# Padding 192-byte rows to a 256-byte pitch in SBUF, in a fused linear-attention and MLP kernel

## The chip, the cores and the metric

One core of one Trainium2 chip. The metric is the device time of one execution in microseconds (us), compared by the median and, where kernels were timed in rounds on the same chip, by ratio. The span in a profile is a little shorter than the device time (198.7 against 200.5 us).

## The reference, cut to what matters

```python
# r, k, v, w: (4, 8, 768, 48) float32; u: (8, 48); x @ w_in: 384 -> 2048; @ w_out: 2048 -> 384
for t in range(S):
    cur = einsum('bhd,bhe->bhde', u[None] * kt, vt)
    y[:, :, t] = einsum('bhd,bhde->bhe', rt, state + cur)
    state = wt[:, :, :, None] * state + einsum('bhd,bhe->bhde', kt, vt)
x = y.transpose(0, 2, 1, 3).reshape(B * S, H * D)
h = maximum(x @ w_in, 0); out = (s * h * h + b) @ w_out
```

The attention is computed in 24 chunks of 128 tokens (4 batches, 6 chunks each). For a chunk, each of w, r, k and v is 128 tokens by 8 heads by 48 floats. In HBM the 48 floats (192 bytes) of a token and head are contiguous, so a load is 1024 rows of 192 B.

## The kernel before

A load writes token t to partition t, the eight heads one after another:

```python
if which == 0:
    c["w"] = ain.tile([128, H, D], FP32, name="wt", tag="wt")          # 8 buffers each
elif which == 1:
    c["rk"] = ain.tile([128, 2, H, D], FP32, name="rkt", tag="rkt")
elif which == 3:
    c["v"] = ain.tile([128, H, D], FP32, name="vt", tag="vt")
...
nc.sync.dma_start(out=dst, in_=src[bb, :, t0 : t0 + L, :].transpose([1, 0, 2]))
```

The readers of these buffers are `ln` (ScalarE, w), `rkp` (GpSimd, r times k), `mult` (VectorE, r and k times the decays), and `yd` and the cast of v (GpSimd). All operations go into a plan, which simulates the engines and ring sizes and puts the instructions in order; attention of later chunks is interleaved with the MLP of earlier ones:

```python
pl = Plan(dict(w=8, rk=8, v=8, lw=NLW, prd=NPR, E=2, RK=RKB, ...))
...
add(("load", n, x), "SP", 0.6, load, (n, x), [], take, 10.0 * n + x, dma=1.03)
```

So a ring size in this dictionary changes the order on every engine. The eight pieces of the MLP weights are loaded after chunk 3, and from chunk 16 on two transposes of each chunk go through the DMA queue too (`RK<-prd` and `xT<-x_sb`), behind the loads.

The softmax here doesn't subtract the row's maximum and nothing guards it: scores larger than these inputs give would overflow.

## Time and profile before

| | before |
|---|---|
| device time, median (range of the first 3 runs) | 200.46 us (198.93 to 201.3) |
| span of the profiled run | 198.7 us |
| PE busy, share of the span | 94% |
| packets of 192 B | 98,304, median 15 ns, 95% under 32 ns |
| w load, issue to landing, median | 4.5 us |

The page divides the span into busy time of each engine (PE is TensorE's matmuls, PEld its weight loads, DVE VectorE, ACT ScalarE, POOL GpSimd). In a row of the windows view, "40.00 (x494)" is 40.00 us busy with 494 instructions in that stretch. A timeline row gives start, duration, engine, line, operation and tiles, then in brackets the idle time ahead of it and what ended that. The figures on packets come from the trace's record of every DMA packet (start, duration, size).

### The profile page before, as it was taken

What the parts mean: (1) busy time and instruction counts of PE and PEld (TensorE: products, weight loads), DVE (VectorE), ACT (ScalarE), POOL (GpSimd) and SP (SyncE); (2) the same over time, 40 slices, a digit from 0 to 9 for tenths busy, and PEclk for the clock granted to TensorE, in tenths of its full rate; (3) what the DMA queues carried; (4) which work ended last, traced back from release to release, by engine and by line L of the source; (5) the groups of instructions that cost most, each with busy time, mean ns of one, the idle gap of its engine ahead of it and who ended that gap; (6) DMA issues with size and microseconds to landing.
All of it is one profiled execution on the core that took longest, in us unless ns stands there. A gap on an engine that the chain in (4) does not pass through costs nothing.

```text
span 198.7 us, 4921 instructions
## 1 busy us (share of the span) xinstructions
PE 187.0 (94%) x1928; PEld 138.9 (70%) x1928; DVE 133.1 (67%) x212; ACT 133.2 (67%) x240; POOL 114.4 (58%) x144
## 2 busy tenths in 40 slices
PE   6997888979999999999999999999999999999992
PEld 4766567745668777777776786776687778777651
DVE  6476838836977978869787686799787692222221
ACT  3446487745658999999996997690069868768000
POOL 3787932029998899959987788959981000000000
PEclk9999999999999999999999999999999999999999
DMA  6999999979999999999999899999433931111122
GB/s 125 200 175 179 299 394 371 278 145 200 188 156 197 160 195 173 200 234 195 220 169 194 186 202 190 210 236 173 128 82 75 122 98 27 43 40 40 43 79 79
DMA packets 119239, 33.29 MB, mean 168 GB/s; under 512 B 112432, under 2 KB 117680, under 8 KB 119216
## 3 DMA queue, kind: packets, MB, share of 16 engines
q1 hardware_dynamic: 119216, 32.98, 83.0%
q8 instruction: 15, 0.25, 0.6%
q14 instruction: 8, 0.07, 0.1%
HBM read 25.36 MB, written 4.72 MB: 151 GB/s over the span
## 4 chain that ended last, share of the span: by engine, by line
PE 66%; DMA 14%; SPq 11%; ACT 3%; POOL 2%; issue 2%; DVE 1%; POOLq 0%
PE o_ps L584 26%; PE h_ps L546 23%; SPq L225 9%; DMA wi_st<-in_moe_w_in_dram 5%; DMA wt<-in_w_dram 5%; DMA rkt<-in_k_dram 4%; PE mt_ps L382 3%; PE o_psh L584 3%; PE trps L340 2%; PE y_ps L419 2%; PE y_ps L410 2%; PE cums L281 1%; PE cums L284 1%; PE d_ps L435 1%; ACT rh L559 1%
## 5 line engine op out<-in xcount | busy, mean ns | idle before, releaser
L546 PE MATMUL h_ps<-xT,w_in 128*128 128x256 bf16 x576 | 73.9, 273 | 2.0 <-ACT w_in L634 1.4
L559 ACT ACTIVATE rh<-h_ps 128x512 bf16<-128x512 f32 x96 | 56.2, 598 | 23.2 <-PE h_ps L546 21.8
L584 PE MATMUL o_ps<-w_out,gT 128*128 128x384 bf16 x352 | 66.3, 326 | 0.0
L546 PEld LDWEIGHTS <-w_in 128*128 128x128 bf16 x576 | 53.7, 98 | 12.5 <-issue 1.8
L584 PEld LDWEIGHTS <-gT 128*128 128x128 bf16 x384 | 35.8, 98 | 19.2
L571 DVE TENSOR_TENSOR gT<-rh 128x512 bf16<-128x512 bf16 x56 | 29.4, 537 | 14.5 <-ACT rh L559 14.4
L237 POOL TENSOR_TENSOR rkp<-rkt 128x384 f32<-128x384 f32 x24 | 25.1, 1047 | 17.2 <-DMA rkt<-in_k_dram 17.1
L394 DVE TENSOR_TENSOR mt_sb<-mt_ps,tri_strict 128x1024 bf16<-128x1024 f32 x24 | 29.2, 1216 | 1.3 <-PE mt_ps L382 1.3
L268 POOL TENSOR_TENSOR yd<-vt,cd 128x384 bf16<-128x384 f32 x24 | 25.2, 1048 | 4.8 <-DVE cd L262 4.6
L313 DVE TENSOR_TENSOR prd<-rkt,E 128x768 bf16<-128x768 f32 x24 | 24.1, 1004 | 5.6 <-ACT E L303 4.1
L569 ACT ACTIVATE gT<-rh 128x512 bf16<-128x512 bf16 x40 | 25.2, 630 | 1.3
L248 POOL TENSOR_TENSOR rku<-rkp,u_bc 128x384 f32<-128x384 f32 x24 | 24.6, 1025 | 0.4
L303 ACT ACTIVATE E<-cums 128x768 bf16<-128x768 f32 x24 | 19.4, 806 | 7.5 <-PE cums L289 7.4
L594 DVE SCALAR_TENSOR_TENSOR o_sb<-o_ps,s_bc,bconst 128x384 f32<-128x384 f32 x22 | 13.5, 615 | 14.8 <-PE o_ps L584 13.4
L486 POOL TENSOR_TENSOR st<-stmp,l 128x384 bf16<-128x384 bf16 x16 | 18.6, 1164 | 8.3 <-DVE stmp L477 7.9
L355 ACT COPY RK<-trps 128x1024 bf16<-128x1024 bf16 x16 | 16.1, 1008 | 5.5 <-PE trps L340 5.5
L449 DVE TENSOR_TENSOR x_sb<-y_ps,yd 128x384 bf16<-128x384 f32 x24 | 13.3, 552 | 6.7 <-PE y_ps L419 5.2
L262 DVE TENSOR_REDUCE cd<-rku 128x8 f32<-128x384 f32 x24 | 13.0, 542 | 6.8 <-POOL rku L248 6.8
L232 ACT ACTIVATE logw<-wt 128x384 bf16<-128x384 f32 x24 | 12.4, 523 | 7.0 <-DMA wt<-in_w_dram 6.8
L816 PE MATMUL warm_ps<-warm_sb 128*128 128x256 bf16 x104 | 15.1, 294 | 1.1 <-DVE warm_sb L795 1.1
L636 POOL CAST vb<-vt 128x384 bf16<-128x384 f32 x24 | 13.4, 558 | 0.0
L816 PEld LDWEIGHTS <-warm_sb 128*128 128x128 bf16 x104 | 10.2, 105 | 2.7 <-DVE warm_sb L795 1.1
(52 smaller groups left out, 168.5 us busy)
## 6 DMA issues: line engine op xcount, KB each, us to landing
wt<-in_w_dram SPq DMA_DIRECT2D x24, 192.0 KB, 4.5
rkt<-in_r_dram SPq DMA_DIRECT2D x24, 192.0 KB, 4.4
rkt<-in_k_dram SPq DMA_DIRECT2D x24, 192.0 KB, 4.6
vt<-in_v_dram SPq DMA_DIRECT2D x24, 192.0 KB, 4.4
out_dram<-o_sb SPq DMA_DIRECT2D x24, 192.0 KB, 2.2
wi_st<-in_moe_w_in_dram SPq DMA_DIRECT2D x4, 768.0 KB, 8.3
wo_st<-in_moe_w_out_dram SPq DMA_DIRECT2D x4, 768.0 KB, 7.6
u_bc<-in_u_dram SPq DMA_DIRECT2D x1, 192.0 KB, 4.3
```

The lines of the kernel that those rows point to most:

```text
L237: nc.gpsimd.tensor_tensor(out=rkp, in0=c["rk"][:, 0].rearrange("t h d -> t (h d)"), in1=c["rk"][:, 1].rearrange("t h d -> t (h d)"), op=AL ...
L248: nc.gpsimd.tensor_tensor(out=rku.rearrange("t h d -> t (h d)"), in0=c["rkp"], in1=u_bc, op=ALU.mult)
L268: nc.gpsimd.tensor_tensor(out=yd, in0=c["v"], in1=c["cd"].unsqueeze(2).to_broadcast([128, H, D]), op=ALU.mult,)
L303: nc.scalar.activation(out=E, in_=ps[:, :, 0:HD], func=AF.Exp)
L313: nc.vector.tensor_tensor(out=prd[:, :, :, 0:D].rearrange("t x h d -> t (x h) d"), in0=c["rk"].rearrange("t x h d -> t (x h) d"), in1=c["E ...
L394: nc.vector.tensor_tensor(out=m.rearrange("s g p t -> s (g p) t"), in0=c["mt_ps"].rearrange("s g p t -> s (g p) t"), in1=tri_strict.unsque ...
L546: nc.tensor.matmul(ps[:, f, :], lhsT=w_in_sb[ft // FPP][:, kt, (ft % FPP) * 128 : (ft % FPP + 1) * 128], rhs=xT[T][:, kt, :], start=(f == ...
L559: nc.scalar.activation(out=rh, in_=hs[T, i], func=AF.Relu)
L569: nc.scalar.activation(out=g, in_=rh, func=AF.Square)
L571: nc.vector.tensor_tensor(out=g, in0=rh, in1=rh, op=ALU.mult)
L584: nc.tensor.matmul(ps, lhsT=gT[T][:, ft, tt * 128 : (tt + 1) * 128], rhs=w_out_sb[ft // FPP][:, ft % FPP, :], start=(ft == 0), stop=(ft == ...
L816: nc.tensor.matmul(warm_ps, lhsT=warm_sb[:, 0:128], rhs=warm_sb, start=True, stop=True)
```

## The change

The intent: rows padded to 256 B in SBUF, so that each 192-byte descriptor lands aligned. As the padded buffers are larger, w gets 5 of them and v gets 7, and the plan is told so.

```diff
-            c["w"] = ain.tile([128, H, D], FP32, name="wt", tag="wt")
+            c["w"] = ain.tile([128, H, 64], FP32, name="wt", tag="wt", bufs=5)[:, :, 0:D]
-            c["rk"] = ain.tile([128, 2, H, D], FP32, name="rkt", tag="rkt")
+            c["rk"] = ain.tile([128, 2, H, 64], FP32, name="rkt", tag="rkt")[:, :, :, 0:D]
-            c["v"] = ain.tile([128, H, D], FP32, name="vt", tag="vt")
+            c["v"] = ain.tile([128, H, 64], FP32, name="vt", tag="vt", bufs=7)[:, :, 0:D]
... (pool1 and pool1b: the same products, written with h and d apart)
-        dict(w=8, rk=8, v=8, lw=NLW, ...
+        dict(w=5, rk=8, v=7, lw=NLW, ...
```

More of the change, by code (lines that the diff above doesn't have):

```diff
@@ L235, in pool1 @@
         c = cb[n]
-        rkp = work.tile([128, HD], FP32, name="rkp", tag="rkp", bufs=2)
+        rkp = work.tile([128, H, D], FP32, name="rkp", tag="rkp", bufs=2)
         nc.gpsimd.tensor_tensor(
             out=rkp,
-            in0=c["rk"][:, 0].rearrange("t h d -> t (h d)"),
-            in1=c["rk"][:, 1].rearrange("t h d -> t (h d)"),
+            in0=c["rk"][:, 0],
+            in1=c["rk"][:, 1],
             op=ALU.mult,
@@ L248, in pool1b @@
         nc.gpsimd.tensor_tensor(
-            out=rku.rearrange("t h d -> t (h d)"), in0=c["rkp"], in1=u_bc, op=ALU.mult
+            out=rku.rearrange("t h d -> t (h d)"),
+            in0=c["rkp"].rearrange("t h d -> t (h d)"),
+            in1=u_bc,
+            op=ALU.mult
         )
@@ L623 @@
     pl = Plan(
-        dict(w=8, rk=8, v=8, lw=NLW, prd=NPR, E=2, RK=RKB, M=3, vb=6, yd=6, x=XSB,
+        dict(w=5, rk=8, v=7, lw=NLW, prd=NPR, E=2, RK=RKB, M=3, vb=6, yd=6, x=XSB,
              cd=4, rkp=2, rku=2, l2=5, A=1, B=2, h=2, o=2, gT=3, xT=XTB, rh=4,
```

## The prediction

0 us for packets, 0 for engine reads, 0 for rings and 0.4 for the order make 200.46 into 200.9, said as 200.8. The "it" of the two checks is the idea that rows off a 256 B boundary cost more. A line through the medians of 65 ns at 1536 B and 84 at 2048 B gives about 15 ns at 192 B (an estimate: 65 less 1344/512 of 19), which is the median measured, so I held that there was nothing left to save. The "floor" of 15 ns is that median (72% of the packets took 13 to 16 ns), and the 0 to +20 ns for an engine's read was a guess.

> **What bounds the kernel now.** I read the windows view first, which gives the busy time of each engine by stretch (its order in a row: PE, PEld, DVE, ACT, POOL, then clock, DMA share, GB/s).
>
> ```profile
> 0.00:20.00 20.00, 17.01 (x178) 12.49 (x179) 12.28 (x24) 9.03 (x15) 13.17 (x24) 1.00 0.97 170
> 20.00:50.00 30.00, 25.90 (x246) 18.66 (x244) 19.42 (x34) 19.69 (x33) 14.22 (x16) 1.00 1.00 281
> 50.00:90.00 40.00, 40.00 (x494) 30.67 (x489) 33.12 (x50) 34.67 (x67) 34.96 (x44) 1.00 1.13 187
> 90.00:110.00 20.00, 19.03 (x221) 14.73 (x219) 16.39 (x26) 17.64 (x36) 17.73 (x22) 1.00 1.15 198
> 110.00:140.00 30.00, 30.00 (x321) 22.33 (x319) 24.09 (x37) 21.47 (x42) 25.33 (x30) 1.00 1.07 196
> 140.00:190.00 50.00, 50.00 (x458) 37.16 (x457) 26.01 (x44) 30.76 (x51) 8.95 (x12) 1.00 0.31 70
> ```
>
> From 50 to 190 us PE idles for 1.0 us (the second row from 90). The DMA engines are full too until 140. Since a busy PE is not a PE at its peak, I checked in the timeline of PE that its groups stand end to start:
>
> ```profile
> 81.33 0.82 PE L546 MATMUL h_ps<-xT,w_in 128*128 128x256 bf16 x6
> 81.99 0.81 PE L584 MATMUL o_ps<-w_out,gT 128*128 128x384 bf16 x4
> 82.73 0.40 PE L382 MATMUL mt_ps<-RK 48*128 48x128 bf16 x8
> 83.06 0.82 PE L584 MATMUL o_ps<-w_out,gT 128*128 128x384 bf16 x4
> 83.72 0.61 PE L340 MATMUL trps<-identity,prd 128*128 128x128 bf16 x8
> ```
>
> Starts are 0.66 us apart after six h_ps (0.109 us a matmul) and four o_ps (0.163 us). With such spacings for every kind, the matmuls in program order after 49.73 us (the mt_ps of chunk 4) sum to about 142.6 us; they end at 195.1, 145.4 us later. So some 3 us of that stretch are stalls. The span of 198.7 us is then: **49.7** us until PE is saturated, **145.4** of nearly solid PE, **3.6** for the last eviction and store. The loads can matter in two ways: through the first term, and by falling behind in the second.
>
> How far ahead they are, from the timelines of the DMA queue and of ScalarE:
>
> ```profile
> 45.32 0.73 SPq L225 DMA_DIRECT2D wt<-in_w_dram  x1
> 49.58 0.52 ACT L232 ACTIVATE logw<-wt 128x384 bf16<-128x384 f32 x1 [0.69 <-DMA wt<-in_w_dram]
> ...
> 103.47 0.94 SPq L225 DMA_DIRECT2D wt<-in_w_dram  x1
> 108.05 0.52 ACT L232 ACTIVATE logw<-wt 128x384 bf16<-128x384 f32 x1 [1.69 <-DMA wt<-in_w_dram]
> ```
>
> For chunk 6, w is issued at 45.3 and read at 49.6, as soon as it lands; for chunk 19 it is 103.5 and 108.1, again with a wait. In between the lead is 4 to 10 us, of which 4.5 are the landing. So loads are **just in time** all the way: they cost PE nothing now, faster ones would give it nothing after 50 us, but clearly slower ones would pass through to it.
>
> [...] Two checks before believing that it binds here:
>
> First, the packet records of the trace. Of 98,304 packets of 192 B, the median took 15 ns, and 72% took 13 to 16 ns. Other median lengths are 18 ns at 256 B, 65 at 1536 B and 84 at 2048 B. [...] The slow 28% (18 to 36 ns) are not particular rows either: several loads that ran with little else in flight have under 2% of them, others 70%, and both kinds follow each other at about 1.0 us a load. I read these as two loads sharing an engine.
>
> Second, the addresses in the built programs. Before, every w, r, k and v buffer begins 224 B past a 256 B boundary, so rows stand 224, 160, 96 and 32 B past one, and three of four cross a boundary. After, the pitch is 256 B but the buffers still begin 224 B past a boundary: **every** row spans 224 to 416 and crosses. The stated intent is not what the program does. [...] The source rows in HBM are as before.
>
> [...] rkp reads flat rows and yd an 8x48 pattern with a broadcast, for the same time.
>
> ```profile
> L237 POOL TENSOR_TENSOR rkp<-rkt 128x384 f32<-128x384 f32 x24 | 25.1, 1047 | 17.2 <-DMA rkt<-in_k_dram 17.1
> L268 POOL TENSOR_TENSOR yd<-vt,cd 128x384 bf16<-128x384 f32 x24 | 25.2, 1048 | 4.8 <-DVE cd L262 4.6
> L636 POOL CAST vb<-vt 128x384 bf16<-128x384 f32 x24 | 13.4, 558 | 0.0
> ```
>
> **The change part by part.**
>
> - *Packets.* Same number, size and source. My estimate of the saving per packet is 0 ns, so loads stay at 64 packets per engine of about 16 ns, 1.03 us. Start: 16 loads before the weights, unchanged, 0 us. Even if every packet took 15 ns (0.96 us a load), 16 loads would give 1.1 us and the first loads after the weights 0.5.
> - *Engine reads.* ln 24 x 523 ns, mult 24 x 1004, rkp 24 x 1047, yd 24 x 1048 and the cast of v 24 x 558 now read at a 256 B pitch. ln and mult already write 64-element rows. I put each at 0 to +20 ns: 24 x 3 x 20 ns is at most 1.4 us on GpSimd, which idles over 3 us in every ten. On the path: 0.
> - *Rings.* w goes from 8 buffers to 5 and v from 8 to 7, which can hold a load back. As loads run at most two or three chunks ahead, the reader that frees the fifth w buffer back is long done: the smallest margin in the trace before is 13 us (w of chunk 14, issued at 80.2 or 15 at 85.4, against the ln of chunks 9 and 10, done at 66.7 and 71.9). For v, seven back, it is 9.4 us (chunk 23: issued at 126.7, chunk 16's yd done at 117.3). No new wait: 0.
> - *Order.* The kernel plans its own order from those rings, so the order changes although the diff does not show it. Comparing the built programs: all engines are the same up to about the load of chunk 12 (some 75 us into the span); after that three stores move ahead of loads and PE interleaves attention and MLP otherwise. PE has the same matmuls. The stores that move up wait for o_sb evictions that ended by 68.5 us in the trace before, so the queue should not block on them. In the tail, the first h_ps of token pair 10 stands about 4.7 us of PE work after the y_ps that it depends on (5.0 before), and that way goes through an addition (0.55), and a DMA transpose (2.3 us to landing). It fits, barely. I allow -1 to +2.5 us, centre +0.4.
>
> Sum: 0 + 0 + 0 + 0.4, so 200.46 becomes 200.9; I say **200.8 us**.
>
> **The rivals.** (1) *Aligned writes were the cost.* Then some of the DMA-full stretch shortens: speaking for it, the DMA share over 1.0 from 50 to 140 and the slow 28%. Against: 15 ns is already the floor, the rows do not become aligned, and PE is solid from 50 us on, so only the start could gain: 1 to 2 us, 199. (2) *The crossing costs on the write side*, now in all rows. [...] Against: the median does not spread over four values[...]. (3) *The new order stalls PE.* The order before was tuned with its rings; a worse fit around the two DMA transposes of the tail, or ScalarE as the bound (34.67 of 40 us from 50 to 90), would make 202 to 204. (4) *The new order is luckier*: at most the 3 us of stalls that are left, 198.
>
> **Range and chances.** Repeated runs of the kernel before spread from 198.93 to 201.3. Adding the order's -1 to +2.5 and some weight for rival 2 gives **197.8 to 204.2**. Faster by over 2% needs 4 us, more than PE's stalls hold unless the start shrinks as well: **0.04**. Slower by over 2% needs rival 2 or a bad case of rival 3: **0.11**. Within 2%: **0.85**.
>
> **What would show it.** Right: 192 B packets still with a median of 15 ns, loads landing in about 4.5 us, weights' first matmul near 25.7 us, PE busy over 138 of 140 us from 50 to 190, GpSimd's means within 20 ns of 1047, 1048 and 558. Rival 1: packets under 15 ns and the chunk 4 cums before 43 us. Rival 2: packets of 17 ns or more, cums of chunk 4 past 46 us, more wait of ScalarE's ln on wt. Rival 3: the start alike and holes in PE after 75 us, with another engine or the transposes as their releaser. A result above 204 or below 197.8 makes me wrong, most likely in the packet term.

## The result, and the profile after

The changed kernel took **213.07 us** (211.91 to 213.5, 4 runs) beside 200.03 us for the kernel before (4 runs): ratio **1.064**, 95% interval 1.056 to 1.072. Ratios here are the mean time of one kernel's fast runs over that of the other's from the same rounds, so not quite the ratio of the medians quoted. The result is correct. The forecast was 200.8 us, with 204.2 as the upper end: clearly wrong.

The windows view of the changed kernel, same stretches and columns as in the prediction:

```profile
0.00:20.00 20.00, 17.88 (x158) 12.83 (x158) 11.50 (x23) 7.57 (x13) 13.11 (x24) 1.00 1.10 154
20.00:50.00 30.00, 24.53 (x244) 18.11 (x244) 18.47 (x33) 19.79 (x33) 12.14 (x15) 1.00 1.01 278
50.00:90.00 40.00, 38.68 (x461) 28.87 (x459) 32.60 (x47) 31.76 (x59) 34.89 (x42) 1.00 1.10 175
90.00:110.00 20.00, 17.76 (x187) 13.85 (x184) 12.32 (x18) 16.60 (x33) 12.03 (x17) 0.91 1.24 177
110.00:140.00 30.00, 28.35 (x305) 20.95 (x302) 23.03 (x37) 24.36 (x47) 27.58 (x34) 1.00 1.15 180
140.00:190.00 50.00, 47.83 (x470) 36.00 (x471) 31.32 (x48) 28.75 (x48) 15.06 (x17) 0.97 0.44 95
```

PE now idles for 7.4 us between 50 and 190 us (1.32 + 2.24 + 1.65 + 2.17), where it idled for 1.0. The DMA engines are about as full as before (shares of 1.10, 1.24 and 1.15 from 50 to 140 us, 1.13, 1.15 and 1.07 before) but move less in the stretches of loads: 175 against 187 GB/s from 50 to 90, 177 against 198, 180 against 196. And the granted clock of PE, 1.00 throughout before, falls to 0.91 and 0.97 in two rows.

The loads themselves, from the DMA queue's timeline of the changed kernel:

```profile
51.78 1.14 SPq L225 DMA_DIRECT2D wt<-in_w_dram  x1
52.97 1.09 SPq L225 DMA_DIRECT2D rkt<-in_r_dram  x1
...
91.30 1.76 SPq L611 DMA_DIRECT2D out_dram<-o_sb  x1
93.16 0.39 SPq L225 DMA_DIRECT2D wt<-in_w_dram  x1
```

In the steady stretch an issue now follows the last after about 1.17 us (it was about 1.03, as at 62.43, 63.53, 64.52 and 65.53 us before): the issues go at about the rate at which such loads drain (1.15 us a load in e1_micro below). From chunk 5 to chunk 23, the w loads were issued 4.64 us apart on average before and 5.04 us after. The last line is the w load of chunk 15, which stands behind a store; e2_align0 below, which has the same order, issues it at 83.47 us, 9.7 us earlier, while its PE is only 4.8 us ahead just before this place.

PE and ScalarE of the changed kernel, at that same w load:

```profile
93.60 1.47 PE L549 MATMUL h_ps<-xT,w_in 128*128 128x256 bf16 x12
...
97.00 0.52 ACT L232 ACTIVATE logw<-wt 128x384 bf16<-128x384 f32 x1 [1.88 <-DMA wt<-in_w_dram]
98.06 2.31 PE L549 MATMUL h_ps<-xT,w_in 128*128 128x256 bf16 x12 [2.14 <-ACT rh L562]
```

`ln` waits 1.88 us for w; the relu behind it on the same engine starts only after it, at 97.43, though the h_ps before it were done at 95.1; and the matmuls that need the relu's buffer wait 2.14 us. The late load reaches PE through an operation that has nothing to do with it. Those twelve h_ps then take 2.31 us, where the twelve at 93.60 took 1.47. In a windows view by 1 us the granted clock is 0.76 from 98 to 99, 0.50 from 99 to 101, 0.53 from 101 to 102, and 1.00 on either side. Half the clock for 3.4 us costs about 1.7 us (an estimate: half of 3.4, the sum of those shortfalls over 0.5).

Over the whole span ScalarE idled for w for 6.8 us before and 13.2 us after (the last number of a row of the lines view, first the kernel before, then the changed one):

```profile
L232 ACT ACTIVATE logw<-wt 128x384 bf16<-128x384 f32 x24 | 12.4, 523 | 7.0 <-DMA wt<-in_w_dram 6.8
L232 ACT ACTIVATE logw<-wt 128x384 bf16<-128x384 f32 x24 | 12.4, 522 | 13.2 <-DMA wt<-in_w_dram 13.2
```

Finally the medians of the DMA issues (out and in, number, KB, us from issue to landing), first before, then after; all four loads land half a microsecond or more later:

```profile
wt<-in_w_dram SPq DMA_DIRECT2D x24, 192.0 KB, 4.5
rkt<-in_r_dram SPq DMA_DIRECT2D x24, 192.0 KB, 4.4
rkt<-in_k_dram SPq DMA_DIRECT2D x24, 192.0 KB, 4.6
vt<-in_v_dram SPq DMA_DIRECT2D x24, 192.0 KB, 4.4
```

```profile
wt<-in_w_dram SPq DMA_DIRECT2D x24, 192.0 KB, 5.0
rkt<-in_r_dram SPq DMA_DIRECT2D x24, 192.0 KB, 5.2
rkt<-in_k_dram SPq DMA_DIRECT2D x24, 192.0 KB, 5.2
vt<-in_v_dram SPq DMA_DIRECT2D x24, 192.0 KB, 5.0
```

Yet the median packet of 192 B still took 15 ns. What grew is the tail: packets over 16 ns went from 28 to 39%, and the mean from 18.2 to 20.6 ns.

### The profile page after: what moved, and what is told of

The parts are those of the page before. It is cut to its first block, busy times and chain, and to the rows that moved or that the text cites. A ratio compares the mean times of both kernels' runs of the same rounds, so it can differ in the third digit from the quotient of the medians.

```text
span 211.2 us, 4914 instructions
## 1 busy us (share of the span) xinstructions
PE 192.6 (91%) x1928; PEld 141.9 (67%) x1928; DVE 134.2 (64%) x212; ACT 134.3 (64%) x240; POOL 114.8 (54%) x144
## 4 chain that ended last, share of the span: by engine, by line
PE 47%; SPq 20%; DMA 19%; ACT 8%; issue 3%; POOL 1%; DVE 0%
PE o_ps L587 20%; PE h_ps L549 18%; SPq L225 18%; DMA wt<-in_w_dram 9%; DMA wi_st<-in_moe_w_in_dram 5%; DMA RK<-prd 4%; ACT rh L562 4%; PE o_psh L587 2%; PE mt_ps L385 2%; ACT RK L358 2%; PE y_ps L422 1%; SPq L520 1%; PE y_ps L413 1%; PE trps L343 1%; ACT gT L572 1%
## 5 line engine op out<-in xcount | busy, mean ns | idle before, releaser
L587 PE MATMUL o_ps<-w_out,gT 128*128 128x384 bf16 x352 | 68.1, 331 | 0.0
L549 PEld LDWEIGHTS <-w_in 128*128 128x128 bf16 x576 | 55.1, 99 | 16.4 <-issue 5.2
L574 DVE TENSOR_TENSOR gT<-rh 128x512 bf16<-128x512 bf16 x56 | 28.3, 513 | 18.6 <-ACT rh L562 18.5
L237 POOL TENSOR_TENSOR rkp<-rkt 128x384 f32<-128x384 f32 x24 | 26.4, 1098 | 19.3 <-DMA rkt<-in_k_dram 19.1
L316 DVE TENSOR_TENSOR prd<-rkt,E 128x768 bf16<-128x768 f32 x24 | 26.0, 1091 | 4.1 <-ACT lam L310 2.0
L271 POOL TENSOR_TENSOR yd<-vt,cd 128x384 bf16<-128x384 f32 x24 | 22.3, 930 | 9.4 <-DVE cd L265 9.3
L248 POOL TENSOR_TENSOR rku<-rkp,u_bc 128x384 f32<-128x384 f32 x24 | 25.1, 1044 | 0.7
L489 POOL TENSOR_TENSOR st<-stmp,l 128x384 bf16<-128x384 bf16 x16 | 18.1, 1133 | 7.4 <-DVE stmp L480 7.3
L232 ACT ACTIVATE logw<-wt 128x384 bf16<-128x384 f32 x24 | 12.4, 522 | 13.2 <-DMA wt<-in_w_dram 13.2
L819 PE MATMUL warm_ps<-warm_sb 128*128 128x256 bf16 x104 | 17.0, 320 | 1.1 <-DVE warm_sb L798 1.1
L385 PE MATMUL mt_ps<-RK 48*128 48x128 bf16 x192 | 9.7, 222 | 5.3 <-DMA RK<-prd 3.8
L819 PEld LDWEIGHTS <-warm_sb 128*128 128x128 bf16 x104 | 11.2, 114 | 3.7 <-DVE warm_sb L798 1.1
```

Of the source, the lines that this page charges most:

```text
L237: nc.gpsimd.tensor_tensor(out=rkp, in0=c["rk"][:, 0], in1=c["rk"][:, 1], op=ALU.mult,)
L248: nc.gpsimd.tensor_tensor(out=rku.rearrange("t h d -> t (h d)"), in0=c["rkp"].rearrange("t h d -> t (h d)"), in1=u_bc, op=ALU.mult)
L271: nc.gpsimd.tensor_tensor(out=yd, in0=c["v"], in1=c["cd"].unsqueeze(2).to_broadcast([128, H, D]), op=ALU.mult,)
L316: nc.vector.tensor_tensor(out=prd[:, :, :, 0:D].rearrange("t x h d -> t (x h) d"), in0=c["rk"].rearrange("t x h d -> t (x h) d"), in1=c["E ...
L549: nc.tensor.matmul(ps[:, f, :], lhsT=w_in_sb[ft // FPP][:, kt, (ft % FPP) * 128 : (ft % FPP + 1) * 128], rhs=xT[T][:, kt, :], start=(f == ...
L574: nc.vector.tensor_tensor(out=g, in0=rh, in1=rh, op=ALU.mult)
```

## The experiments

**Theories.** *Crossing*: a row that crosses a 256 B boundary of SBUF (it has bytes on both sides of an address that is a multiple of 256) costs more to write; after the change all rows cross, before it three of four. *Gap*: rows that don't follow one another in SBUF cost more, wherever they stand. *Order*: the loads are slow or late because the smaller rings made a worse order. The boundary positions come from the addresses in the built programs: all load buffers begin 224 B past a boundary, before and after.

### e1_micro: loads alone, thirteen layouts

Everything but loads was taken out (the result is wrong). Eight loads go back to back into one buffer, then VectorE reads the buffer, then comes the next layout; all thirteen layouts, then again in reverse.

```python
VARIANTS = [  # (bytes of the first row past a 256 B boundary, bytes from row to row)
    (224, 192), (224, 256), (0, 256), (64, 256), (32, 256), (128, 256),
    (0, 192), (0, 224), (0, 208), (16, 256), (0, 512), (224, 512), (0, 320)]
```

> Wrong result on purpose: nothing but loads of the kernel's own kind (1024 rows of 192 B), eight at a time into one buffer, 13 layouts of the destination, each twice (the second pass in reverse), with a reduction between groups. Per load, from the packets of a group: layout of before (first row 224 B past a 256 B boundary, pitch 192) about 1.0 us. Crossing theory[...]: 224/256 1.15 to 1.2 us, 128/256 the same, while 0/256, 64/256 and 32/256, which don't cross, take 0.95 to 1.0 us, and 0/192 (two of four rows cross) is no slower than before. Gap theory (rows that don't follow one another cost, wherever they stand): every pitch over 192 takes about 1.15 us, 0/192 as 224/192. If all take about 1.0 us, the cost needs the rest of the kernel around it.

The time of a load is worked out from the packets: the time from the start of the packet at 10% of a group to that at 90%, scaled to 1024 packets; the two numbers are the two passes.

| first row / pitch | rows that cross | us a load | duration of a packet, mean ns |
|---|---|---|---|
| 224 / 192 (before) | 3 of 4 | 0.99, 1.00 | 20.5, 20.1 |
| 224 / 256 (after) | all | 1.15, 1.15 | 24.2, 25.0 |
| 128 / 256 | all | 1.15, 1.15 | 25.5, 25.7 |
| 224 / 512 | all | 1.15, 1.15 | 24.7, 25.1 |
| 0 / 224 | 5 of 8 | 0.93, 0.93 | 18.4, 18.1 |
| 0 / 208 | 5 of 8 | 0.97, 0.94 | 17.1, 16.9 |
| 0 / 192 | 2 of 4 | 0.92, 0.92 | 15.3, 15.3 |
| 0, 16, 32, 64 / 256 | none | 0.85 to 0.93 | 15.2 to 15.5 |
| 0 / 320 | 2 of 4 | 0.88, 0.91 | 15.7, 15.3 |
| 0 / 512 | none | 0.90, 0.91 | 15.2, 15.5 |

(The last column is taken over all packets of a group.) The crossing theory holds and the gap theory falls: a pitch of 256 costs nothing while no row crosses, even for rows that start 16, 32 or 64 B past a boundary (0.85 to 0.93 us a load). Where a crossing row stands made no difference in the two cases here: 128/256 and 224/256 both took 1.15 us.

What a load of each kind looks like as a rate: the DMA view of this run, first in the 10 us of a group of 224/256, then in the 9 us of a group of 0/256 (40 equal slices of each window).

```profile
GB/s 0 0 0 0 0 8 109 151 246 239 200 187 190 184 168 198 194 181 168 171 166 166 164 156 167 167 162 161 164 164 166 164 159 166 164 164 164 159 167 162
```

```profile
GB/s 0 0 0 0 7 102 94 190 257 243 253 248 224 172 177 230 238 246 218 241 244 207 240 242 217 208 250 260 252 244 241 258 199 196 200 248 108 35 5 0
```

Both begin near 245 GB/s; the crossing group then sinks to about 164 and stays there, the other stays between 172 and 260 until its last packets, mostly above 200. The packets show the same: cutting a group of 224/256 into eighths by packet order, the share of packets over 16 ns is 0.00, 0.16, 0.53, 0.83, 0.87, 0.90, 0.91, 0.90; for 224/192 it is 0.01, 0.00, 0.32, 0.60, 0.66, 0.75, 0.80, 0.76; for 0/256 and 0/192 never above 0.01. So the packets at the start of a burst are fast in all four layouts, and where rows cross they grow slow as the burst goes on; what lies behind this, no run here shows. The trace of the kernel before has the same pattern: over eight loads from a pause at about 80 us, the share over 16 ns goes 0.00, 0.03, 0.03, 0.24, 0.49, 0.67, 0.71, 0.78.

### e2_align0 and e3_align64: the changed kernel, moved by 32 and by 96 bytes

Small pads ahead of the load buffers and behind them, so that only these buffers move against a boundary; order and rings are those of the changed kernel.

```diff
+        if n == 0 and which == 0:
+            nc.gpsimd.memset(ain.tile([128, 8], FP32, name="xpad", tag="xpad", bufs=1), 0.0)
         if which == 0:
             c["w"] = ain.tile([128, H, 64], FP32, name="wt", tag="wt", bufs=5)[:, :, 0:D]
... (behind the v tile: a pad of 56 floats; e3: 24 floats ahead and 40 behind)
```

> The changed kernel with 32 B put ahead of the load buffers (and 224 B behind, so that nothing else moves against a 256 B boundary): rows of w, r, k and v now truly start on 256 B boundaries. Crossing theory: the loads come down to about 1.0 us each or less, and the time to 199 to 203 us (what is left over before is the order's). Gap theory: loads stay at 1.15 us and the time at 212 to 214 us.

> As the one before, but rows start 64 B past a boundary and end on the next: no row crosses, none starts on one. Crossing theory: the same as e2_align0 within 1 us. If the start itself must stand on a boundary: loads about 1.1 us or more, and 208 us or more. Gap theory: 212 to 214 us.

e2 took 198.95 us (198.41 to 200.3), ratio to before 0.989 (0.983 to 0.994); e3 198.92 us (198.63 to 200.24), ratio 0.989 (0.984 to 0.994). The move alone is worth some 14 us against the changed kernel, whose profiled span was 211.2 us against 196.9 here (the two were not timed in the same rounds; each one's ratio to before, 1.064 and 0.989, says the same). Rows that begin on a boundary and rows that end on one do equally well (198.95 and 198.92 us): it is the crossing. Two views of e2_align0, windows and DMA issues:

```profile
50.00:90.00 40.00, 40.00 (x500) 31.12 (x498) 33.94 (x52) 34.80 (x67) 36.05 (x44) 1.00 0.98 201
90.00:110.00 20.00, 20.00 (x223) 15.73 (x221) 17.75 (x24) 18.64 (x38) 16.95 (x21) 1.00 1.05 218
110.00:140.00 30.00, 30.00 (x331) 22.37 (x330) 23.94 (x38) 20.56 (x38) 27.67 (x34) 1.00 0.77 163
```

```profile
wt<-in_w_dram SPq DMA_DIRECT2D x24, 192.0 KB, 3.7
rkt<-in_r_dram SPq DMA_DIRECT2D x24, 192.0 KB, 3.7
```

PE has no idle time left in these stretches, the DMA moves 201 GB/s from 50 to 90 us and 218 from 90 to 110, and a load lands in 3.7 us (5.0 in the changed kernel, 4.5 before). ScalarE idled for w for 2.4 us in all. The packets of 192 B took 15 ns at the median and 15 ns at 95%: the tail is gone.

As PE's instruction stream is the same in e2 and in the changed kernel, the two can be laid over each other. The lag of the changed kernel's `cums` matmuls (one pair a chunk):

| | chunk 1 | 6 to 10 | 11 | 13 | 14 to 20 | 21 to 23 | last o_sb eviction |
|---|---|---|---|---|---|---|---|
| lag, us | 1.8 | 2.5 | 4.3 | 4.8 | 8.8 | 14.3 | 14.3 |

The 14.3 us are a few steps. The start: 2.5 us for the loads of the first chunks (the first h_ps, behind the weights, starts at 27.57 us against 25.27). Chunks 11 to 13: 2.3 us. The place at 98 us shown above: 4.0 us, of which 2.14 are the gap and about 1.7 the halved clock. And 5.5 us between chunks 20 and 21, where PE of the changed kernel waits for the DMA transposes (a timeline of PE, then two rows of the windows view of PE alone, in which the clock stands after PE's count):

```profile
140.17 0.40 PE L385 MATMUL mt_ps<-RK 48*128 48x128 bf16 x8 [1.82 <-DMA RK<-prd]
...
145.00 0.40 PE L385 MATMUL mt_ps<-RK 48*128 48x128 bf16 x8 [2.00 <-DMA RK<-prd]
145.51 2.00 PE L549 MATMUL h_ps<-xT,w_in 128*128 128x256 bf16 x12
```

```profile
140.00:145.00 5.00, 2.83 (x36) 1.00 1.23 195
145.00:150.00 5.00, 5.00 (x49) 0.66 0.51 115
```

These transposes stand in the queue behind the last loads, which are issued until 138 us (v of chunk 23 at 137.86). The first of these four was issued at 135.51, and in e2 at 120.44: 15.1 us apart, where PE was 8.8 apart. The two gaps make 3.8 us. After the first the clock stayed at 1.00 until 146; after the second it was halved again (0.66 over 5 us is about 3.4 us at half; 0.50 from 147 to 149), some 1.7 us more by the same estimate. So the gaps of 2.14 and 2.00 us were each followed by a halved clock and that of 1.82 us was not; what sets it, three gaps do not show.

### e4_rings_only: the rings and the order alone

```diff
-            c["w"] = ain.tile([128, H, D], FP32, name="wt", tag="wt")
+            c["w"] = ain.tile([128, H, D], FP32, name="wt", tag="wt", bufs=5)
-            c["v"] = ain.tile([128, H, D], FP32, name="vt", tag="vt")
+            c["v"] = ain.tile([128, H, D], FP32, name="vt", tag="vt", bufs=7)
-        dict(w=8, rk=8, v=8, lw=NLW, ...
+        dict(w=5, rk=8, v=7, lw=NLW, ...
```

> The layout of before (rows of 192 B one after another) with the rings of the changed kernel (w 5, v 7 buffers), hence its order: the built programs agree instruction by instruction on all engines. If the loads' own cost makes the difference: 199 to 203 us, loads at 1.0 us. If the new order makes it: 210 us or more with loads at 1.0 us. The prediction said +0.4 us for this part.

200.18 us (199.91 to 201.01), ratio 0.993 (0.989 to 0.998), loads landing in 4.4 to 4.6 us. The smaller rings and the new order cost nothing; they gain 0.7%. The order theory falls. This run also settles a side question. The means of two readers of r and k had gone up in the changed kernel (rkp from 1047 to 1098 ns, mult, whose tile is prd, from 1004 to 1091). Here, with packed rows and that order, rkp is:

```profile
L237 POOL TENSOR_TENSOR rkp<-rkt 128x384 f32<-128x384 f32 x24 | 26.7, 1113 | 17.1 <-DMA rkt<-in_k_dram 17.1
```

and mult 1104 ns. So those went up with the order, not with the pitch.

### e5_micro2: what the cost of a crossing depends on

Loads alone again (a wrong result): shorter and longer rows, and rows of `moe_w_in` that begin 0 or 128 B past a boundary in HBM.

```python
VARIANTS = [  # (source, bytes of a row, first row past a boundary, pitch)
    ("h", 192, 0, 256), ("h", 192, 224, 256), ("h", 96, 0, 256), ("h", 96, 208, 256),
    ("h", 32, 0, 256), ("h", 32, 240, 256), (0, 192, 0, 256), (0, 192, 224, 256),
    (128, 192, 0, 256), (128, 192, 224, 256), (0, 256, 0, 512), (0, 256, 128, 512)]
```

> Wrong result on purpose, loads alone again: what a crossing row's cost depends on. If each piece of a row on either side of a 256 B boundary is one write and a write costs about 9 ns (17.9 ns a crossing row in e1_micro), the crossing layouts take about 1.15 us a load whatever the row's length: 96 B (at 208) and 32 B (at 240) as 192 B (at 224) and 256 B (at 128). [...] Source: the four layouts from moe_w_in tell whether reading rows that cross a boundary in HBM costs too: if the read side sets the 0.9 us of the layouts that don't cross (two of four source rows of w cross), rows at 0 with a destination at 0 take clearly less than 0.9 us and rows at 128 clearly more; if reads are free of it, all with a destination at 0 take about 0.9 us.

| bytes of a row, source | no row crosses in SBUF, us | every row crosses, us |
|---|---|---|
| 32, heads of w, r, k, v | 0.74, 0.78 | 1.06, 1.06 |
| 96, heads | 0.80, 0.81 | 1.11, 1.11 |
| 192, heads | 0.89, 0.93 | 1.15, 1.15 |
| 192, weights from 0 B (no source row crosses) | 0.97, 0.89 | 1.16, 1.15 |
| 192, weights from 128 B (every source row crosses) | 0.90, 0.94 | 1.15, 1.15 |
| 256, weights | 1.03, 1.09 | 1.16, 1.16 |

A load of crossing rows of 32 B is nearly as dear as one of 256 B (1.06 and 1.16 us): in these runs the time of crossing rows goes with the number of pieces into which boundaries cut the rows, hardly with bytes. Taken over the second half of each group, after the burst at the start, the crossing columns read 1.16 to 1.22 us for all lengths. Reading rows that cross in HBM cost nothing that shows (0.90 and 0.94 us with every source row crossing, 0.97 and 0.89 with none). A cost that goes with the bytes, with short crossing rows as fast as short ones that don't cross: 1.06 against 0.74 and 0.78 us rules it out. Of the two outcomes that I had set out for the source, the second came: with an aligned destination all 192-byte rows took 0.89 to 0.97 us. The miss was in the short rows: I expected 1.15 us for all that cross, and over the whole group those of 32 B took 1.06.

A small model fits, an estimate from these runs. Spread evenly over the 16 DMA engines of the page, a load is 64 rows an engine, and each piece then takes 9 ns (1.15 us / 64 / 2). Rows that all cross need 128 pieces, 1.15 us. With three of four crossing it is 112 pieces, 1.01 us by this model and 0.99 to 1.00 measured. With five of eight it is 104, 0.93 us, and measured 0.93 (pitch 224) and 0.94 to 0.97 (pitch 208). With two of four it is 96, 0.86 us, which falls under the 0.85 to 0.93 us that loads take anyway, and measured 0.92. This is a fit to these runs; that anything writes in such pieces, no run here shows.

### e6_shift_only: the kernel before, moved by 32 bytes

Same pads as in e2, with the pitch of 192 B, the rings and the order of before. Two of four rows cross.

> The kernel before (pitch 192, its rings and its order, the built programs agree on every engine but for two small memsets) with the load buffers moved by 32 B: rows stand 0, 192, 128 and 64 B past a boundary, two of four cross, where three of four did. From e1_micro (0/192: 0.92 us a load against 0.99): loads at about 0.95 us and 3.6 to 3.8 us to landing, the time 198 to 200 us, 0.5 to 1.5% under before. If the smaller rings or the other order made the gain of e2_align0: 200 to 202 us.

200.11 us (199.41 to 200.91), ratio 0.995 (0.990 to 1.000), 5 rounds. The loads did get faster as expected (3.7 to 4.0 us to landing, 15 ns at 95% of the packets), and the time by a little; the interval just reaches 1, so the gain of the shift alone is likely and not shown.

### e7_rk_cross: half the dose, in the order of before

Only r and k padded, nothing moved, rings 8, 8, 8: all rows of r and k cross, three of four of w and v.

> The order and the rings of before with only r and k padded to 256 B rows, not shifted: half of the loads have every row crossing (1.15 us), the other half three of four (1.0 us). The order is that of before instruction by instruction. Crossing theory: 203 to 208 us, r and k loads slower to land; if the slowdown needed the new order or rings: 199 to 202 us.

204.41 us (204.02 to 204.83), ratio 1.017 (1.009 to 1.024). Slower with the old order and old rings, so neither is needed for the slowdown. Half of the loads made slow cost about a quarter of the whole: I take it that some of a late load is still taken up by the slack ahead of its reader, which no run here tests.

### e8_shift_plan: an order made for the faster loads

```diff
-            add(("load", n, x), "SP", 0.6, load, (n, x), [], take, 10.0 * n + x, dma=1.03)
+            add(("load", n, x), "SP", 0.6, load, (n, x), [], take, 10.0 * n + x, dma=0.96)
```

> e6_shift_only with the plan told that a load takes 0.96 us where it said 1.03, so that the order is made for the faster loads. If PE's order is what keeps e6 from gaining more: 196 to 198.5 us. If PE's own work is the bound from 50 us on: as e6 within 1 us.

201.35 us (200.87 to 202.5), ratio 1.002 (0.995 to 1.008): no gain over e6, if anything a loss. Loads landed as fast as in e6 (3.7 to 3.9 us). A better figure in the plan did not give a better order. That PE's work is the bound fits (PE is busy for all but 0.2 us from 50 to 190 us), but e8 came 1.2 us above e6 where I had allowed 1, and its profiled run has a granted clock of 0.94 from 20 to 50 us, so this run alone does not show it.

### e9_shift_rings and e10_align0_again: the best version

e9 is e4 with the pads of e2: packed rows, two of four crossing, rings and order of the changed kernel. e10 is e2 again beside it.

> Pitch 192 as before, load buffers moved by 32 B (two of four rows cross), and the rings and order of the changed kernel: the cheap half of both. If the padding itself earns nothing beyond two crossings in four: the same as e2_align0 within 1 us, 198.5 to 199.5 us on that chip, 1.1% under before. If full alignment is worth more in the kernel than in the loads alone: 200 us or more.

> e2_align0 again, beside e9 on the same chip and with more rounds: 0.987 to 0.992 of before, if its gain was no accident of that chip.

e9 took 198.75 us (198.08 to 200.24), ratio 0.990 (0.984 to 0.996); e10 198.51 us (198.12 to 199.59), ratio 0.987 (0.982 to 0.993). Their intervals overlap widely. Both beat the kernel before, by 1.0 and 1.3%; both beat the changed kernel by some 7% (by the ratios to before; they were not timed beside it). The padding itself buys nothing that these runs can tell from packed rows whose buffers begin on a boundary, and e9 needs 14,336 B less SBUF per partition.

## Why the prediction was wrong, point by point

- **What bounds the kernel: right.** PE was the bound from 50 us on, and loads ran just in time, so that "clearly slower ones would pass through" to PE. They did, through the relu that stands behind `ln` on ScalarE and through the DMA transposes. Rival 1's limit on what faster loads could give (1 to 2 us) also held as far as can be told: e6 gained 0.5%, with an interval that reaches 1; e10 gained 1.3%, of which e4 puts 0.7% down to rings and order.
- **The packet term failed, and the whole miss is in it.** The step took the median duration of a packet (15 ns) for its cost, and so put 0 us where the change cost 0.15 us or more on each load: 0.99 or 1.00 us became 1.15 in e1_micro (1.05 became 1.21 over the second half of the group), and in the kernel issues went from about 1.03 to 1.17 us apart. The median stayed 15 ns all the same, as it did in the changed kernel. Fast packets at the start of each burst hide the cost; it shows in the mean (18.2 to 20.6 ns) and in the rate. The line through the packet lengths was loose as well: its 65 ns for 1536 B is the median of the stores alone. The loads of that size took 68 and all together 66, and with 68 the same line gives 26 ns for a 192 B packet, not 15 (both estimates from the medians).
- **The tail was put down to the wrong cause.** "The slow 28% ... I read these as two loads sharing an engine": they go with crossing rows, late in a burst. With two of four rows crossing, or none, packets over 16 ns all but vanish (about 1% of a group in e1_micro, but for one pass of 0/320 with up to 13% in an eighth; 15 ns at 95% in e2 and e6), with as many loads in flight. The loads with under 2% of them, which I took as proof against the rows, were those after a pause of the queue, as at 80 us above and at the start of every group in e1_micro. I had used a difference between loads to acquit a property of rows, without asking how packets of the same rows look early and late in a burst.
- **The addresses: right, and the decisive observation.** "Every row spans 224 to 416 and crosses." The change did the opposite of its intent because the pool began 224 B past a boundary.
- **Rival 2: right about the crossing, wrong in its size.** Rows that cross do cost on the way into SBUF. The loads alone show 0.15 to 0.16 us (0.99 or 1.00 to 1.15), the same for 128/256 as for 224/256, and in e5_micro2 the cost goes with the pieces (1.06 us a load for crossing rows of 32 B, 1.16 for 256 B). The rival was given too little weight because of the packet step. "The median does not spread over four values" was no evidence against it: the median was 15 ns after the change too. Two of the three signs that I had set for it did not show although it was right: the median packet stayed at 15 ns (17 or more foreseen) and the cums of chunk 4 came at 45.5 us (past 46 foreseen). Only the wait of `ln` for w did, 6.8 us before and 13.2 after.
- **Loads unchanged at the start (0 us): wrong by 1.9 us.** The first h_ps moved from 25.70 to 27.57 us.
- **Engine reads (0 to +20 ns): right in what they say of pitch.** The cast of v went from 558 to 565 ns. rkp and mult rose by 51 and 87 ns, and yd fell by 118, but e4 has 1113, 1104 and 955 ns with packed rows: the order, which the step had not allowed for. That GpSimd "idles over 3 us in every ten" was misread too: from 50 to 90 us it idles 5.0 of 40.
- **Rings (0) and order (+0.4 us, -1 to +2.5): small, as foreseen.** Together they gave -0.7%, some -1.3 us, in e4, a little below the range, though the interval (-1.1 to -0.2%) reaches into it. The tail's transposes that "fit, barely" did so while loads were fast (e2, e4) and cost 5.5 us when they were not.

## What to carry to other kernels

Alignment is a matter of addresses, not of pitch: read the built program for where a buffer begins before padding its rows, since a pitch of 256 B on a base that is off turns some crossings into all of them (ratio to before 1.064 here, and 0.989 with the base moved by 32 B). When many small rows go to SBUF, count the rows that cross a 256 B boundary (in e1_micro 0.85 to 0.93 us a load with none crossing, 1.15 with all); packed rows of 192 B on an aligned base were as good here as padded ones (ratios of 0.990 and 0.987). And judge a transfer by its rate over a full queue, not by the median duration of its packets: that was 15 ns before and after, while the loads alone went from 0.99 or 1.00 to 1.15 us.
